# Fetching f, k and q in rows of four tokens: 64 token groups stand twice on the partitions

## The chip, the cores and the metric

The kernel runs on one core of one Trainium2 chip. The metric is the device time of one execution in microseconds (us). The kernel before took 827.85 us, the median of three runs (826.41 to 830.13).

## What is computed

Three layers follow each other. The first, and the only one that the change touches, is a gated linear attention over 4 batches, 8 heads, 768 tokens and 48 channels per head:

```python
f = 1.0 / (1.0 + np.exp(-f_logit))
state = np.zeros((B, H, D, D), dtype=np.float32)
for t in range(S):
    state = f[:, :, t, :, None] * state + np.einsum('bhd,bhe->bhde', k[:, :, t], v[:, :, t])
    y[:, :, t] = np.einsum('bhd,bhde->bhe', q[:, :, t], state)
```

Its output, as 3072 rows of 384 values, goes to a mixture of 8 experts (each takes 384 tokens, in the order of a gate's logits) and then to a dense layer with a gated activation. All inputs are float32, in HBM. f, k, q and v lie as [batch, head, token, channel], so that neighbouring tokens of one head are neighbours in memory and heads are 768 x 48 values apart.

## The kernel before

The attention function works on units of U=256 tokens of one batch (12 units, three per batch), each as two chunks of 128 tokens (24 chunks, j in the code). Its instructions are written out by hand, engine by engine: the loop over j interleaves the matrix work of chunk j with the preparation of unit j//2+2, by small closures (`slot`, `refill`). Every engine runs its own queue strictly in the order written. DMAs of this part are all issued by SP, in order: `later` collects the loads and the stores of x that are issued at the next flush.

**Loading and regrouping (L62 to L87).** `load` brings one unit of f, k or q into a tile `fr`, `kr` or `qr` [128, 8 heads, 96]: partition p holds tokens 2p and 2p+1 of the unit, which are 96 values or 384 bytes in one piece, for each head. Each of the three tiles has one buffer, so the next unit's load is issued only when the readers of the present one are done. f goes through Tanh (L77) and a scale (L78) on ACT into `ft`; DVE multiplies the f of the two tokens (L79) into `pmf`; k and q are spread into `pmk` and `pmq` as two planes, one for each of the two tokens: in one, k is multiplied by the second token's f (L82) and q by the first's (L86), and the other plane is copied by ACT (L83, L87). In these tiles a pair of heads fills 2 x 64 columns (48 used).

**Transposing and scaling.** PE transposes each [128 groups, pair of heads] block into `pT` in PSUM: `decays` for f (L92), `turned` for k and q (L113), the two planes interleaved. DVE scans the products of f along the tokens (L99, L107) and scales q and k with them (L126). What follows works on transposed tiles [channels of a pair, tokens]: scores (L146), the state's part of y (L152), y (L203), the update of the state (L214 to L222).

**Output.** `l_mm` (L228) turns y back to [tokens, 384] and computes the gate's logits in the same product; ACT copies y out (L233), SP stores it to `x_dram` (L234). Beside all this SP also loads v (L71) and, for the layers behind, the weights `pw` (L947) and `wo` (L966), which DVE, ACT and POOL unpack a piece per slot.

The change touches `load`, `decay`, `keys`, `queries`, `decays`, `turned`, the head number in `y_mm` and `kv_mm`, the copy in `l_mm` and the gate weight's load at L240. Everything behind `x_dram` stays.

Of the kernel before, what the change touches and what calls it, by code (L numbers as in the profile page):

```python
# [17 lines left out]
def attention(tc, q,k,v,f,wg, x_dram, lg, ident, pmin, ranges, prep, setup, spin):  # L18
    nc=tc.nc
    ctx=ExitStack()  # L20
    with ctx:
        ld=ctx.enter_context(tc.tile_pool(name="ald",bufs=2))
        cs=ctx.enter_context(tc.tile_pool(name="acs",bufs=1))
        wk=ctx.enter_context(tc.tile_pool(name="awk",bufs=2))
        ps=ctx.enter_context(tc.tile_pool(name="aps",bufs=1,space=PS))
        perm={'f':cs.tile([128,NP,2,64],F32,name="pmf")}
        nc.vector.memset(perm['f'][:,:,:,48:],1.0)
        for nm in 'kq':
            t=cs.tile([128,2,NP,2,64],F32,name=f"pm{nm}")
            nc.vector.memset(t[:,:,:,:,48:],0.0)  # L30
            perm[nm]=t
        half=cs.tile([128,1],F32,name="half"); nc.vector.memset(half,0.5)
        ft=cs.tile([128,2,H,D],F32,name="ft")
        L=G+1; W2=4*L
        held=ps.tile([128,512],F32,name="pC"); m0=held[:,:W2-1]; m1=held[:,512-W2:]
        nc.vector.memset(held,0.0)
# [15 lines left out]
        FF=[]
        for i in range(2):
            t=cs.tile([128,W2+4],F32,name=f"ff{i}"); nc.gpsimd.memset(t,0.0); FF.append(t)
        for t in VP: nc.gpsimd.memset(t[:,:,:,D:],0.0)
        nc.gpsimd.memset(SW,0.0)
        for s in range(2):
            for o in range(2):
                b=(s^o)*D
                nc.gpsimd.tensor_copy(SW[64*s:64*s+48,o::2,b:b+D],ident[64*s:64*s+48,None,64*s:64*s+D].to_broadcast([48,NP//2,D]))  # L60
        raw={}
        def load(u,nm,h0=0,h1=H):  # L62
            b,o=divmod(u*U,S)
            if nm!='v':
                src={'f':f,'k':k,'q':q}[nm]
                t=ld.tile([128,H,2*D],F32,name=nm+"r",bufs=1) if h0==0 else raw[nm,u]
                nc.sync.dma_start(t[:,h0:h1],bass.AP(tensor=src.tensor,offset=src.offset+b*H*S*D+h0*S*D+o*D,ap=[[2*D,128],[S*D,h1-h0],[1,2*D]]))
            else:
                t=VP[u%2]
                for c in range(2):  # L70
                    nc.sync.dma_start(t[:,c,:,:D],bass.AP(tensor=v.tensor,offset=v.offset+b*H*S*D+(o+c*C)*D,ap=[[D,C],[S*D,H],[1,D]]))  # L71
            raw[nm,u]=t
        view=lambda u,nm: raw[nm,u].rearrange("p h (r d) -> p r h d",d=D)
        home=lambda nm,r: perm[nm][:,r].rearrange("p a s d -> p (a s) d")[:,:,:48]
        def decay(u,i,h0=0,h1=H):
            x=ft[:,:,h0:h1]
            if i==0: nc.scalar.activation(x,view(u,'f')[:,:,h0:h1],AF.Tanh,scale=0.5)  # L77
            elif i==1: nc.scalar.activation(x,x,AF.Identity,bias=half[:,0:1],scale=0.5)  # L78
            else: nc.vector.tensor_mul(perm['f'].rearrange("p a s d -> p (a s) d")[:,h0:h1,:48],ft[:,0,h0:h1],ft[:,1,h0:h1])  # L79
        def keys(u,i,h0=0,h1=H):  # L80
            x=view(u,'k')[:,:,h0:h1]
            if i==0: nc.vector.tensor_mul(home('k',0)[:,h0:h1],x[:,0],ft[:,1,h0:h1])  # L82
            else: nc.scalar.copy(home('k',1)[:,h0:h1],x[:,1])  # L83
        def queries(u,i,h0=0,h1=H):
            x=view(u,'q')[:,:,h0:h1]
            if i==0: (nc.vector if u else nc.gpsimd).tensor_tensor(out=home('q',0)[:,h0:h1],in0=x[:,0],in1=ft[:,0,h0:h1],op=OP.mult)  # L86
            else: nc.scalar.copy(home('q',1)[:,h0:h1],x[:,1])  # L87
        KH={};QT={};PC={};PX={};SX={}
        V=nc.vector
        def decays(u,pairs):  # L90
            pt=ps.tile([128,512],F32,name="pT",bufs=PB).rearrange("p (a c g) -> p a c g",a=NP,c=2)
            for p in pairs: nc.tensor.transpose(pt[:,p].rearrange("p c g -> p (c g)"),perm['f'][:,p].rearrange("p a d -> p (a d)"),ident)  # L92
            for h in sorted({p//2 for p in pairs}):
                ff=FF[h][:,:W2].rearrange("p (a c g) -> p a c g",a=2,c=2)
                nc.scalar.copy(ff[:,:,:,1:],pt[:,2*h:2*h+2])
        flat=lambda t: t.rearrange("p a c g -> p (a c g)")
# [10 lines left out]
            V.tensor_tensor_scan(flat(SX[u,h])[:,1:][:,::-1],FF[h][:,2:W2+1][:,::-1],m1[:,1:][:,::-1],0.0,op0=OP.mult,op1=OP.max)  # L107
        PT={}
        def turned(u,nm,h):
            pt=ps.tile([128,512],F32,name="pT",bufs=PB).rearrange("p (a g r) -> p a g r",a=2,r=2)  # L110
            for a in range(2):
                for r in range(2):
                    nc.tensor.transpose(pt[:,a,:,r],perm[nm][:,r,2*h+a].rearrange("p s d -> p (s d)"),ident)  # L113
            PT[u,nm,h]=pt
        def scaled(u,nm,h):
            if nm=='k': o=KH[u]=KHB[u%2]
            elif h==0: o=QT[u]=wk.tile([128,NP,U],F32,name="qt")
# [20 lines left out]
        AM={};KT={};pA={}  # L138
# [51 lines left out]
        def y_mm(j,part):  # L190

            u,c=divmod(j,2); first=j%6==0
            vr=raw['v',u]; last=j==NCH-1
            rows=[slice(64*s,64*s+64) for s in range(2)]
            if part==0:
                if last: PY[j]=[ps.tile([128,NP,C],F32,name=f"pA{i}") for i in range(2)]
                else: PY[j]=[ps.tile([128,NP,C],F32,name="pT",bufs=PB) for _ in range(1 if first else 2)]*(2 if first else 1)
                return
            yt=wk.tile([128,NP,C],F32,name="yt")
            for p in (0,2,1,3):  # L200
                py=PY[j][p%2]
                for s in range(2):
                    nc.tensor.matmul(py[rows[s^p%2],p],vr[:,c,2*p+s],AM[j][:,s,p],start=first,stop=first or p>1)  # L203
                if p>1 and not first: nc.scalar.copy(yt[:,p%2::2],py[:,p%2::2])
            if first: nc.scalar.copy(yt,py)
            YT[j]=yt
        def kv_mm(j):
            u,c=divmod(j,2); first=j%6==0
            if j%6==5 or j>=NCH: return
            vr=raw['v',u]  # L210
            pk=ps.tile([128,512],F32,name="pT",bufs=PB)[:,:NP*D].rearrange("p (a d) -> p a d",a=NP)
            for p in range(NP):
                for s in range(2):
                    nc.tensor.matmul(pk[64*s:64*s+64,p],KT[j][:,p,s],vr[:,c,2*p+s,:D],start=True,stop=True)  # L214
            sn=St[(j+1)%2][:,:,:D]; so=St[j%2][:,:,:D]
            def update():
                pcb=PC[u][:,:,c][:,:,None].to_broadcast([128,NP,D])
                if first:
                    nc.vector.tensor_tensor(out=sn,in0=pk,in1=pcb,op=OP.mult)
                else:  # L220
                    nc.vector.tensor_add(so,so,pk)
                    nc.gpsimd.tensor_tensor(out=sn,in0=so,in1=pcb,op=OP.mult)  # L222
            late.append(update)
        def l_mm(j):
            W=2*D+8
            px=ps.tile([128,512],F32,name="pT",bufs=PB)[:,:NP*W].rearrange("p (a e) -> p a e",a=NP)
            for p in (0,2,1,3):
                nc.tensor.matmul(px[:,p],YT[j][:,p],SW[:,p],start=True,stop=True)  # L228
            y=wk.tile([128,NP,2*D],F32,name="y")
            def logits(): nc.vector.tensor_reduce(lg[:,j],px[:,:,2*D:].rearrange("p a e -> p e a"),axis=AX.X,op=OP.add)  # L230
            if j==NCH-1: logits()
            else: late.append(logits)
            nc.scalar.copy(y,px[:,:,:2*D])  # L233
            later.append(lambda: nc.sync.dma_start(x_dram[j*C:(j+1)*C,:],y.rearrange("p a d -> p (a d)")))  # L234
        ranges=ranges(lambda: ps.tile([128,384],F32,name="pT",bufs=PB),lambda: ps.tile([128,512],F32,name="pT",bufs=PB))
        for h in (0,4):
            for nm in 'fqk': load(0,nm,h,h+4)
        load(0,'v')
        for s in range(2):
            for o in range(2): nc.sync.dma_start(SW[64*s:64*s+48,o::2,2*D:],wg.rearrange("(p s d) e -> s d p e",p=NP,s=2)[s^o][:,o::2])  # L240
        WARM=(4,1,8)
        def warm(n):

            t=ps.tile([128,512],F32,name="pT",bufs=PB)
            for _ in range(n): nc.tensor.matmul(t[:,:128],ident,ident,start=True,stop=True)
        warm(WARM[0])
        lo,hi=(0,4),(4,8)
        for i in range(3): decay(0,i,*lo)
        decays(0,(0,1))
        for i in range(2): queries(0,i,*lo)  # L250
# [19 lines left out]
        for nm in 'fqk': load(1,nm)  # L270
# [652 lines left out]
def gla_moe_ffn(tc,q,k,v,f_logit,moe_w_gate,moe_w1,moe_w2,moe2_w_in,moe2_w_out,out):  # L923
    nc=tc.nc
    with ExitStack() as ctx:
# [133 lines left out]
        with tc.tile_pool(name="prep",bufs=1) as pi:  # L1059
            attention(tc,q,k,v,f_logit,moe_w_gate,x_dram,lg,ident,pmin,ranges,both(prep_in(pi),prep_out(pi,wr0,0,NOUT,3,512)),lambda: (rt.constants(),p0),rt.spin)  # L1060
# [103 lines left out]
```

## Time and profile before

| | |
|---|---|
| median of three runs | 827.85 us |
| the profiled execution's own time | 825.67 us |
| its span, first to last instruction | 824.0 us |
| PE busy in the span | 789.4 us (96%) |
| DVE busy | 547.4 us (66%) |
| ACT busy | 365.4 us (44%) |
| q1 (SP's DMA queue): packets, bytes | 95872, 73.96 MB |

The attention part fills about the first 150 us. Shares over the whole span mix it with the expert layers, where PE is busy nearly all the time; what the change is worth is read from the first 150 us alone, engine by engine. A DMA share over 1 in a stretch means that packets of one DMA engine overlap.

### The profile page before, as it was taken

How to read it: one execution, taken by the hardware profiler on the slowest of the kernel's cores; microseconds unless marked ns; L12 is line 12 of the kernel's file. 1: busy time of each engine (PE TensorE's matmuls, PEld its weight loads, DVE VectorE, ACT ScalarE, POOL GpSimd, SP SyncE). 2: the span in 40 equal slices, each digit the busy share in tenths (PEclk: the TensorE clock that was granted, in tenths of full speed). 3: DMA queues.
4: the chain of work that ended last, by engine and by line, in shares of the span. 5: the costliest groups of instructions: out<-in, count | busy, mean ns of one | idle time of the engine just before them, and what ended most of it. 6: DMA issues, size and time to landing. Idle time of an engine off the chain costs nothing.

```text
span 824.0 us, 16675 instructions
## 1 busy us (share of the span) xinstructions
PE 789.4 (96%) x6385; PEld 757.4 (92%) x6385; DVE 547.4 (66%) x1517; ACT 365.4 (44%) x757; POOL 125.5 (15%) x215
## 2 busy tenths in 40 slices
PE   7989999879999999999999999999999999999994
PEld 6878898769999999899999999999999999999994
DVE  6999999767797468648855866587756524642431
ACT  5877786242455144415431643254235424541431
POOL 2556543120011001101010001100300020010001
PEclk9999999969999999999999999999999999999998
DMA  9999984550034013203322322322213332331000
GB/s 225 228 257 253 275 236 119 176 191 1 1 88 123 1 37 104 91 20 122 110 74 68 97 85 78 95 87 84 91 63 97 89 99 72 97 97 39 1 1 33
DMA packets 99032, 84.54 MB, mean 103 GB/s; under 512 B 67328, under 2 KB 86912, under 8 KB 98944
## 3 DMA queue, kind: packets, MB, share of 16 engines
q1 hardware_dynamic: 95872, 73.96, 31.9%
q0 software_dynamic: 3072, 9.44, 3.6%
q8 instruction: 52, 0.85, 0.4%
q14 instruction: 36, 0.29, 0.1%
HBM read 73.94 MB, written 9.44 MB: 101 GB/s over the span
## 4 chain that ended last, share of the span: by engine, by line
PE 59%; issue 10%; DVE 7%; DMA 2%; ACT 1%; POOL 1%; SPq 0%; POOLq 0%; DVEq 0%; ACTq 0%
PE acc L736 10%; PE pF L736 10%; PE acc L737 9%; PE acc L738 9%; PE pF L737 9%; PE pF L738 9%; DVE ga L881 1%; DVE hl L884 1%; DVE w1l L785 1%; PE pF L823 1%; POOL out_dram L915 1%; DMA xg<-x_dram,q_ids 1%; ACT hh L883 1%; DMA wst<-in_moe_w_dram 1%; DMA xh<-in_moe_w_dram 1%
## 5 line engine op out<-in xcount | busy, mean ns | idle before, releaser
L881 DVE SCALAR_TENSOR_TENSOR ga<-ga,pF 128x384 f32<-128x384 f32 x128 | 70.8, 553 | 100.0 <-ACT ga L879 99.6
L736 PE MATMUL acc<-wo,hh 128*128 128x384 f32 x384 | 132.9, 346 | 1.0 <-ACT hh L883 1.0
L736 PE MATMUL pF<-xh,wih 128*128 128x384 f32 x384 | 131.6, 343 | 0.0
L737 PE MATMUL acc<-wo,hl 128*128 128x384 f32 x384 | 129.6, 337 | 0.4 <-DVE hl L884 0.4
L737 PE MATMUL pF<-xh,wil 128*128 128x384 f32 x384 | 129.4, 337 | 0.0
L738 PE MATMUL acc<-wo,hh 128*128 128x384 f32 x384 | 129.3, 337 | 0.0
L738 PE MATMUL pF<-xl,wih 128*128 128x384 f32 x384 | 129.3, 337 | 0.0
L879 ACT ACTIVATE ga<-pF,three 128x384 f32<-128x384 f32 x128 | 74.3, 582 | 105.3 <-PE pF L738 101.0
L883 ACT CAST hh<-ga 128x384 fp32r<-128x384 f32 x128 | 65.8, 514 | 88.6 <-DVE ga L881 86.2
L844 ACT ACTIVATE hh<-pF 128x384 fp32r<-128x384 f32 x64 | 31.5, 492 | 131.5 <-PE pF L738 118.6
L915 POOL DMA_INDIRECT out_dram<-ga,q_ids x24 | 24.2, 1010 | 385.5 <-ACT ga L913 382.5
L884 DVE TENSOR_TENSOR hl<-ga,hh 128x384 fp32r<-128x384 f32 x128 | 71.0, 555 | 13.4 <-ACT hh L883 9.8
L845 DVE SCALAR_TENSOR_TENSOR hl<-pF,hh 128x384 fp32r<-128x384 f32 x64 | 35.5, 555 | 65.6 <-ACT hh L844 65.3
L736 PEld LDWEIGHTS acc<-wo,hh 128*128 128x128 f32 x384 | 72.1, 188 | 2.2 <-ACT hh L883 1.3
L737 PEld LDWEIGHTS acc<-wo,hl 128*128 128x128 f32 x384 | 72.2, 188 | 1.8 <-DVE hl L884 1.8
L737 PEld LDWEIGHTS pF<-xh,wil 128*128 128x128 f32 x384 | 72.2, 188 | 0.0
L736 PEld LDWEIGHTS pF<-xh,wih 128*128 128x128 f32 x384 | 72.2, 188 | 0.0
L738 PEld LDWEIGHTS pF<-xl,wih 128*128 128x128 f32 x384 | 72.1, 188 | 0.0
L738 PEld LDWEIGHTS acc<-wo,hh 128*128 128x128 f32 x384 | 72.0, 188 | 0.0
L736 PE MATMUL pF<-xh,w1h 128*128 128x384 f32 x192 | 66.6, 347 | 0.6 <-ACT xh L814 0.6
L736 PE MATMUL acc<-hh,w2h 128*128 128x384 f32 x192 | 66.1, 344 | 0.0
L737 PE MATMUL pF<-xh,w1l 128*128 128x384 f32 x192 | 64.8, 338 | 0.0
(285 smaller groups left out, 1605.9 us busy)
## 6 DMA issues: line engine op xcount, KB each, us to landing
wst<-in_moe_w_dram SPq DMA_DIRECT2D x58, 192.0 KB, 2.5
wst<-in_moe_w_dram SPq DMA_DIRECT2D x42, 256.0 KB, 2.9
pw<-in_moe_w_in_dram SPq DMA_DIRECT2D x12, 512.0 KB, 6.3
wo<-in_moe_w_out_dram SPq DMA_DIRECT2D x16, 384.0 KB, 7.3
pm<-in_moe_w_out_dram SPq DMA_DIRECT2D x32, 192.0 KB, 2.4
pm<-in_moe_w_in_dram SPq DMA_DIRECT2D x30, 192.0 KB, 2.5
v<-in_v_dram SPq DMA_DIRECT2D x24, 192.0 KB, 5.2
x_dram<-y SPq DMA_DIRECT2D x24, 192.0 KB, 4.5
```

The source lines that it names most:

```text
L736: nc.tensor.matmul(out, ahi, bhi, start=start, stop=False)
L737: nc.tensor.matmul(out, alo, bhi, start=False, stop=False)
L738: nc.tensor.matmul(out, ahi, blo, start=False, stop=stop)
L785: nc.vector.tensor_tensor(out=lo,in0=got[i],in1=hi.bitcast(F32),op=OP.subtract)
L823: nc.tensor.transpose(p[:,h*128:(h+1)*128],s.xg[:,h,d*128:(d+1)*128],s.ident)
L844: nc.scalar.activation(hh,p,AF.Relu)
L845: s.defer(2,lambda: nc.vector.scalar_tensor_tensor(hl,p,0.0,hh.bitcast(F32),op0=OP.max,op1=OP.subtract))
L879: nc.scalar.activation(a,p,AF.Relu,bias=s.three[:,0:1])
L881: late(f,n1,lambda: nc.vector.scalar_tensor_tensor(g,a,6.0,p,op0=OP.min,op1=OP.mult))
L883: late(f,n2,lambda: nc.scalar.copy(gh,g))
L884: late(f,n3,lambda: nc.vector.tensor_tensor(out=gl,in0=g,in1=gh.bitcast(F32),op=OP.subtract))
L915: st=nc.gpsimd.indirect_dma_start(out=s.out,out_offset=bass.IndirectOffsetOnAxis(ap=ids[:,t:t+1],axis=0),in_=o,in_offset=None)
```

## The change

f, k and q are fetched in rows of four tokens, 192 values or 768 bytes in one piece. A unit of 256 tokens has 64 such groups, and they stand twice on the partitions: partitions 0 to 63 hold heads 0 to 3, partitions 64 to 127 heads 4 to 7. So each load becomes two DMAs of 64 partitions and four heads each. A pair of heads for the transposes is now made of heads of one half, and a transposed block holds both halves side by side: `turned` does the four tokens of a group one by one, for two pairs at a time, and writes every fourth column of `pT` (every second before); `decays` writes every second column (each column before). The number of heads behind a pair and a side is `head(p,s)`; the copy of y puts the pairs back in the order of the output.

```diff
+        ft=cs.tile([128,4,4,D],F32,name="ft")
...
+        head=lambda p,s: 4*(p%2)+2*(p//2)+s
+        def load(u,nm,h0=0,h1=4):
...
-                t=ld.tile([128,H,2*D],F32,name=nm+"r",bufs=1) if h0==0 else raw[nm,u]
-                nc.sync.dma_start(t[:,h0:h1],bass.AP(tensor=src.tensor,offset=src.offset+b*H*S*D+h0*S*D+o*D,ap=[[2*D,128],[S*D,h1-h0],[1,2*D]]))
+                t=ld.tile([128,4,4*D],F32,name=nm+"r",bufs=1) if h0==0 else raw[nm,u]
+                for g in range(2):
+                    nc.sync.dma_start(t[64*g:64*g+64,h0:h1],bass.AP(tensor=src.tensor,offset=src.offset+b*H*S*D+(4*g+h0)*S*D+o*D,ap=[[4*D,64],[S*D,h1-h0],[1,4*D]]))
...
+        home=lambda nm,r: perm[nm][:,r::2,:,:48]
...
-            else: nc.vector.tensor_mul(perm['f'].rearrange("p a s d -> p (a s) d")[:,h0:h1,:48],ft[:,0,h0:h1],ft[:,1,h0:h1])
+            else: nc.vector.tensor_mul(perm['f'][:,:,h0:h1,:48],ft[:,0::2,h0:h1],ft[:,1::2,h0:h1])
...
-            if i==0: nc.vector.tensor_mul(home('k',0)[:,h0:h1],x[:,0],ft[:,1,h0:h1])
+            if i==0: nc.vector.tensor_mul(home('k',0)[:,:,h0:h1],x[:,0::2],ft[:,1::2,h0:h1])
...
-            for p in pairs: nc.tensor.transpose(pt[:,p].rearrange("p c g -> p (c g)"),perm['f'][:,p].rearrange("p a d -> p (a d)"),ident)
+            for h in halves:
+                for i in range(2):
+                    nc.tensor.transpose(pt[:,2*h:2*h+2].rearrange("p b c (g i) -> p b (c g) i",i=2)[:,:,:,i],perm['f'][:,i,2*h:2*h+2].rearrange("p s d -> p (s d)"),ident)
...
-            for a in range(2):
-                for r in range(2):
-                    nc.tensor.transpose(pt[:,a,:,r],perm[nm][:,r,2*h+a].rearrange("p s d -> p (s d)"),ident)
+            for i in range(4):
+                nc.tensor.transpose(pt.rearrange("p (a g i) -> p a g i",a=2,i=4)[:,:,:,i],perm[nm][:,i,2*h:2*h+2].rearrange("p s d -> p (s d)"),ident)
...
-            nc.scalar.copy(y,px[:,:,:2*D])
+            nc.scalar.copy(y.rearrange("p (b a) d -> p a b d",b=2),px[:,:,:2*D].rearrange("p (a b) d -> p a b d",b=2))
...
-        for h in (0,4):
-            for nm in 'fqk': load(0,nm,h,h+4)
+        for h in (0,2):
+            for nm in 'fqk': load(0,nm,h,h+2)
```

On PE, ACT, DVE and POOL the order and the number of instructions stay, only shapes and waits differ. On SP each load of f, k and q is now two issues. The first rows of SP's queue before (names are the tile written and the input read, then the shape written; the waits are for earlier DMAs, which share eight semaphores in turn, and for readers of the buffer):

```order
L67 DMA fr<-in_f_logit_dram 128x4x96
L67 DMA qr<-in_q_dram 128x4x96
L67 DMA kr<-in_k_dram 128x4x96
L67 DMA fr<-in_f_logit_dram 128x4x96
L67 DMA qr<-in_q_dram 128x4x96
L67 DMA kr<-in_k_dram 128x4x96
L71 DMA v_111<-in_v_dram 128x8x48 x2
L240 DMA sw<-in_moe_w_gate_dram 48x2x8 [waits DMAHW0_49,Pool_49]
L240 DMA sw<-in_moe_w_gate_dram 48x2x8 [waits DMAHW1_49]
L240 DMA sw<-in_moe_w_gate_dram 48x2x8 [waits DMAHW2_49]
L240 DMA sw<-in_moe_w_gate_dram 48x2x8 [waits DMAHW3_49]
L67 DMA fr<-in_f_logit_dram 128x8x96 [waits DMAHW4_49,Activation_49]
```

The same stretch of SP's queue now, from the second part of unit 0 to the load of f for unit 1 (line numbers are two to five higher there):

```order
L69 DMA fr<-in_f_logit_dram 64x2x192 x2
L69 DMA qr<-in_q_dram 64x2x192 [waits DMAHW0_49]
L69 DMA qr<-in_q_dram 64x2x192 [waits DMAHW1_49]
L69 DMA kr<-in_k_dram 64x2x192 [waits DMAHW2_49]
L69 DMA kr<-in_k_dram 64x2x192 [waits DMAHW3_49]
L73 DMA v_111<-in_v_dram 128x8x48 [waits DMAHW4_49]
L73 DMA v_111<-in_v_dram 128x8x48 [waits DMAHW5_49]
L244 DMA sw<-in_moe_w_gate_dram 48x2x8 [waits DMAHW6_49,Pool_49]
L244 DMA sw<-in_moe_w_gate_dram 48x2x8 [waits DMAHW7_49]
L244 DMA sw<-in_moe_w_gate_dram 48x2x8 [waits DMAHW0_49]
L244 DMA sw<-in_moe_w_gate_dram 48x2x8 [waits DMAHW1_49]
L69 DMA fr<-in_f_logit_dram 64x4x192 [waits DMAHW2_49,Activation_49]
```

Unit 0 takes twelve issues instead of six (in two parts of half the heads), and the v, gate and unit-1 loads stand behind them.

On DVE the same instructions stand in the same places; the ones that read `qr` and `kr` wait for two DMAs instead of one. Before, in the preparation of unit 2:

```order
L79 TENSOR_TENSOR pmf<-ft 128x8x48 [waits Activation_49]
L219 TENSOR_TENSOR St_117<-pT,pmin 128x4x48 [waits PE_49]
L937 TENSOR_SCALAR pm<-pw 128x512 [waits DMAHW7_49]
L86 TENSOR_TENSOR pmq<-qr,ft 128x8x48 [waits DMAHW2_49]
L126 TENSOR_TENSOR kh_114<-pT,S 128x512 [waits DVE_49,PE_49]
L939 SCALAR_TENSOR_TENSOR pm<-pw,pm 128x512 [waits DVE_49]
L82 TENSOR_TENSOR pmk<-kr,ft 128x8x48 [waits DMAHW3_49]
```

The same place now:

```order
L81 TENSOR_TENSOR pmf<-ft 128x8x48 [waits Activation_49]
L223 TENSOR_TENSOR St_117<-pT,pmin 128x4x48 [waits PE_49]
L941 TENSOR_SCALAR pm<-pw 128x512 [waits DMAHW0_49]
L88 TENSOR_TENSOR pmq<-qr,ft 128x2x4x48 [waits DMAHW5_49,DMAHW4_49]
L130 TENSOR_TENSOR kh_114<-pT,S 128x512 [waits DVE_49,PE_49]
L943 SCALAR_TENSOR_TENSOR pm<-pw,pm 128x512 [waits DVE_49]
L84 TENSOR_TENSOR pmk<-kr,ft 128x2x4x48 [waits DMAHW7_49,DMAHW6_49]
```

Nothing moved here; the shapes have one dimension more and two rows one wait more.

## Rows read from the trace of the kernel before

**Rows 1.** The page: DVE's busy tenths in 40 slices of the span; DMA packets by size.
```profile
DVE  6999999767797468648855866587756524642431
...
DMA packets 99032, 84.54 MB, mean 103 GB/s; under 512 B 67328, under 2 KB 86912, under 8 KB 98944
```

**Rows 2.** Busy time of each engine in two stretches of 25 us, clock, DMA share.
```profile
core 0: us, PE busy (x) PEld busy (x) DVE busy (x) ACT busy (x) POOL busy (x), PEclk, DMA share, GB/s
25.00:50.00 25.00, 24.36 (x468) 22.12 (x457) 24.86 (x50) 19.68 (x46) 16.27 (x25) 1.00 0.94 240
75.00:100.00 25.00, 22.59 (x382) 19.70 (x379) 23.86 (x52) 18.76 (x44) 15.23 (x22) 1.00 1.00 271
```

**Rows 3.** What DVE waited for, 25 to 150 us: total, times, longest.
```profile
DVE St L221 <- PE pT L214: 4.0, 6, 1.1
DVE pm L937 <- DMA wo<-in_moe_w_out_dram: 0.5, 1, 0.5
```

**Rows 4.** Timeline of SP, start of the kernel: start, duration (idle before, what ended it).
```profile
0.81 0.44 SPq L67 DMA_DIRECT2D fr<-in_f_logit_dram  x1
...
3.50 0.51 SPq L67 DMA_DIRECT2D kr<-in_k_dram  x1
4.05 2.41 SPq L71 DMA_DIRECT2D v<-in_v_dram  x2
6.57 2.53 SPq L240 DMA_DIRECT2D sw<-in_moe_w_gate_dram  x4
9.20 0.38 SPq L67 DMA_DIRECT2D fr<-in_f_logit_dram  x1
```

**Rows 5.** Timeline of ACT: the Tanh of f (units 1 and 2) and the step behind it.
```profile
12.87 0.84 ACT L77 ACTIVATE ft<-fr 128x768 f32<-128x768 f32 x1 [1.15 <-DMA fr<-in_f_logit_dram]
...
19.96 0.84 ACT L77 ACTIVATE ft<-fr 128x768 f32<-128x768 f32 x1 [1.40 <-DMA fr<-in_f_logit_dram]
...
41.41 0.94 ACT L78 ACTIVATE ft<-ft,half 128x768 f32<-128x768 f32 x1
```

**Rows 6.** Timeline of DVE: the product of f's two tokens (units 1, 2 and 4).
```profile
14.71 0.56 DVE L79 TENSOR_TENSOR pmf<-ft 128x384 f32<-128x384 f32 x1 [1.10 <-ACT ft L78]
...
22.15 0.56 DVE L79 TENSOR_TENSOR pmf<-ft 128x384 f32<-128x384 f32 x1 [0.66 <-ACT ft L78]
...
45.05 0.88 DVE L79 TENSOR_TENSOR pmf<-ft 128x384 f32<-128x384 f32 x1
```

**Rows 7.** DMA packets in 2.5:3.5 and 18.5:21.5 (f, k, q), and 15.25:17 (pw).
```profile
DMA packets 801, 0.30 MB, mean 298 GB/s; under 512 B 801, under 2 KB 801, under 8 KB 801
...
DMA packets 2052, 0.79 MB, mean 264 GB/s; under 512 B 2051, under 2 KB 2051, under 8 KB 2051
...
DMA packets 187, 0.70 MB, mean 400 GB/s; under 512 B 16, under 2 KB 16, under 8 KB 187
```

**Rows 8.** Transposes in 25:125, by line: busy, mean ns of one.
```profile
L113 PE MATMUL pT<-ident,pmq 128*128 128x128 f32 x72 | 11.3, 280 | 0.0
L92 PE MATMUL pT<-ident,pmf 128*128 128x128 f32 x32 | 4.9, 275 | 1.7 <-DVE pmf L79 1.0 <-ACT kt L187 0.7
```

**Rows 9.** Timeline of SP: the row on each side of two idle stretches.
```profile
35.38 0.71 SPq L234 DMA_DIRECT2D x_dram<-y  x1
38.53 0.34 SPq L947 DMA_DIRECT2D pw<-in_moe_w_in_dram  x1
...
47.03 0.54 SPq L234 DMA_DIRECT2D x_dram<-y  x1
50.28 0.34 SPq L947 DMA_DIRECT2D pw<-in_moe_w_in_dram  x1
```

**Rows 10.** Two instructions whose shapes change, 0 to 155 us, by line.
```profile
L86 DVE TENSOR_TENSOR pmq<-qr,ft 128x384 f32<-128x384 f32 x11 | 8.4, 759 | 0.0
...
L233 ACT COPY y<-pT 128x384 f32<-128x384 f32 x24 | 11.7, 488 | 4.7 <-PE pT L228 1.9 <-DVE lg L230 1.1 <-ACT yt L204 1.0
```

**Rows 11.** DMA issues of f, count, size, us to landing, 0 to 155 us.
```profile
fr<-in_f_logit_dram SPq DMA_DIRECT2D x11, 384.0 KB, 5.3
```

More of the change, by code (lines that the diff above doesn't have):

```diff
@@ L25, in attention @@
         ps=ctx.enter_context(tc.tile_pool(name="aps",bufs=1,space=PS))
-        perm={'f':cs.tile([128,NP,2,64],F32,name="pmf")}
+        perm={'f':cs.tile([128,2,NP,64],F32,name="pmf")}
         nc.vector.memset(perm['f'][:,:,:,48:],1.0)
         for nm in 'kq':
-            t=cs.tile([128,2,NP,2,64],F32,name=f"pm{nm}")
-            nc.vector.memset(t[:,:,:,:,48:],0.0)
+            t=cs.tile([128,4,NP,64],F32,name=f"pm{nm}")
+            nc.vector.memset(t[:,:,:,48:],0.0)
             perm[nm]=t
         half=cs.tile([128,1],F32,name="half"); nc.vector.memset(half,0.5)
-        ft=cs.tile([128,2,H,D],F32,name="ft")
+        ft=cs.tile([128,4,4,D],F32,name="ft")
         L=G+1; W2=4*L
@@ L61, in attention @@
         raw={}
-        def load(u,nm,h0=0,h1=H):
+        head=lambda p,s: 4*(p%2)+2*(p//2)+s
+        def load(u,nm,h0=0,h1=4):
             b,o=divmod(u*U,S)
@@ L73, in attention, with decay @@
         view=lambda u,nm: raw[nm,u].rearrange("p h (r d) -> p r h d",d=D)
-        home=lambda nm,r: perm[nm][:,r].rearrange("p a s d -> p (a s) d")[:,:,:48]
-        def decay(u,i,h0=0,h1=H):
+        home=lambda nm,r: perm[nm][:,r::2,:,:48]
+        def decay(u,i,h0=0,h1=4):
             x=ft[:,:,h0:h1]
@@ L78, in decay, with keys, queries @@
             elif i==1: nc.scalar.activation(x,x,AF.Identity,bias=half[:,0:1],scale=0.5)
-            else: nc.vector.tensor_mul(perm['f'].rearrange("p a s d -> p (a s) d")[:,h0:h1,:48],ft[:,0,h0:h1],ft[:,1,h0:h1])
-        def keys(u,i,h0=0,h1=H):
+            else: nc.vector.tensor_mul(perm['f'][:,:,h0:h1,:48],ft[:,0::2,h0:h1],ft[:,1::2,h0:h1])
+        def keys(u,i,h0=0,h1=4):
             x=view(u,'k')[:,:,h0:h1]
-            if i==0: nc.vector.tensor_mul(home('k',0)[:,h0:h1],x[:,0],ft[:,1,h0:h1])
-            else: nc.scalar.copy(home('k',1)[:,h0:h1],x[:,1])
-        def queries(u,i,h0=0,h1=H):
+            if i==0: nc.vector.tensor_mul(home('k',0)[:,:,h0:h1],x[:,0::2],ft[:,1::2,h0:h1])
+            else: nc.scalar.copy(home('k',1)[:,:,h0:h1],x[:,1::2])
+        def queries(u,i,h0=0,h1=4):
             x=view(u,'q')[:,:,h0:h1]
-            if i==0: (nc.vector if u else nc.gpsimd).tensor_tensor(out=home('q',0)[:,h0:h1],in0=x[:,0],in1=ft[:,0,h0:h1],op=OP.mult)
-            else: nc.scalar.copy(home('q',1)[:,h0:h1],x[:,1])
+            if i==0: (nc.vector if u else nc.gpsimd).tensor_tensor(out=home('q',0)[:,:,h0:h1],in0=x[:,0::2],in1=ft[:,0::2,h0:h1],op=OP.mult)
+            else: nc.scalar.copy(home('q',1)[:,:,h0:h1],x[:,1::2])
         KH={};QT={};PC={};PX={};SX={}
@@ L91, in decays @@
             pt=ps.tile([128,512],F32,name="pT",bufs=PB).rearrange("p (a c g) -> p a c g",a=NP,c=2)
-            for p in pairs: nc.tensor.transpose(pt[:,p].rearrange("p c g -> p (c g)"),perm['f'][:,p].rearrange("p a d -> p (a d)"),ident)
-            for h in sorted({p//2 for p in pairs}):
+            halves=sorted({p//2 for p in pairs})
+            for h in halves:
+                for i in range(2):
+                    nc.tensor.transpose(pt[:,2*h:2*h+2].rearrange("p b c (g i) -> p b (c g) i",i=2)[:,:,:,i],perm['f'][:,i,2*h:2*h+2].rearrange("p s d -> p (s d)"),ident)
+            for h in halves:
                 ff=FF[h][:,:W2].rearrange("p (a c g) -> p a c g",a=2,c=2)
@@ L109, in turned @@
         def turned(u,nm,h):
-            pt=ps.tile([128,512],F32,name="pT",bufs=PB).rearrange("p (a g r) -> p a g r",a=2,r=2)
-            for a in range(2):
-                for r in range(2):
-                    nc.tensor.transpose(pt[:,a,:,r],perm[nm][:,r,2*h+a].rearrange("p s d -> p (s d)"),ident)
-            PT[u,nm,h]=pt
+            pt=ps.tile([128,512],F32,name="pT",bufs=PB)
+            for i in range(4):
+                nc.tensor.transpose(pt.rearrange("p (a g i) -> p a g i",a=2,i=4)[:,:,:,i],perm[nm][:,i,2*h:2*h+2].rearrange("p s d -> p (s d)"),ident)
+            PT[u,nm,h]=pt.rearrange("p (a g r) -> p a g r",a=2,r=2)
         def scaled(u,nm,h):
@@ L202, in y_mm @@
                 for s in range(2):
-                    nc.tensor.matmul(py[rows[s^p%2],p],vr[:,c,2*p+s],AM[j][:,s,p],start=first,stop=first or p>1)
+                    nc.tensor.matmul(py[rows[s^p%2],p],vr[:,c,head(p,s)],AM[j][:,s,p],start=first,stop=first or p>1)
                 if p>1 and not first: nc.scalar.copy(yt[:,p%2::2],py[:,p%2::2])
@@ L213, in kv_mm @@
                 for s in range(2):
-                    nc.tensor.matmul(pk[64*s:64*s+64,p],KT[j][:,p,s],vr[:,c,2*p+s,:D],start=True,stop=True)
+                    nc.tensor.matmul(pk[64*s:64*s+64,p],KT[j][:,p,s],vr[:,c,head(p,s),:D],start=True,stop=True)
             sn=St[(j+1)%2][:,:,:D]; so=St[j%2][:,:,:D]
@@ L232, in l_mm @@
             else: late.append(logits)
-            nc.scalar.copy(y,px[:,:,:2*D])
+            nc.scalar.copy(y.rearrange("p (b a) d -> p a b d",b=2),px[:,:,:2*D].rearrange("p (a b) d -> p a b d",b=2))
             later.append(lambda: nc.sync.dma_start(x_dram[j*C:(j+1)*C,:],y.rearrange("p a d -> p (a d)")))
         ranges=ranges(lambda: ps.tile([128,384],F32,name="pT",bufs=PB),lambda: ps.tile([128,512],F32,name="pT",bufs=PB))
-        for h in (0,4):
-            for nm in 'fqk': load(0,nm,h,h+4)
+        for h in (0,2):
+            for nm in 'fqk': load(0,nm,h,h+2)
         load(0,'v')
         for s in range(2):
-            for o in range(2): nc.sync.dma_start(SW[64*s:64*s+48,o::2,2*D:],wg.rearrange("(p s d) e -> s d p e",p=NP,s=2)[s^o][:,o::2])
+            for o in range(2): nc.sync.dma_start(SW[64*s:64*s+48,o::2,2*D:],wg.rearrange("(o a s d) e -> s o d a e",o=2,a=2,s=2)[s^o][o])
         WARM=(4,1,8)
@@ L246, in attention @@
         warm(WARM[0])
-        lo,hi=(0,4),(4,8)
+        lo,hi=(0,2),(2,4)
         for i in range(3): decay(0,i,*lo)
```

## The prediction

> **What bounds the kernel now.** I read the page first, then the busy time by stretches, then what DVE waited for, then the timelines of the first 25 us, engine by engine, and last the DMA packets.
>
> The page's slices (20.6 us each) show DVE at nine tenths or more in the second to fourth, and 7 or more to the seventh [rows 1]. By stretches DVE is busy 24.86 of 25 us from 25 to 50, and 23.86 from 75 to 100, while ACT is at 19 to 20 and PE's weight loads at 20 to 22 [rows 2]. From 25 us on, what DVE waits for is PE and one load of `wo`, 4.5 us in all, and never f, k or q [rows 3]. So the attention part is bound by DVE's own instructions, in an order written by hand, from 25 us to its end. The DMA engines are nearly as full (0.94 and 1.00 [rows 2]), which makes the change look promising, but a full resource that nobody waits for is not the bound; 67328 of 99032 packets are under 512 bytes [rows 1].
>
> Before 25 us it is different. ACT's Tanh of f waits for the load in unit 1 (1.15 us) and unit 2 (1.40) [rows 5], and DVE behind it waits 1.10 and 0.66 us [rows 6]. Whatever shifts DVE there shifts all that follows, since DVE has no idle time later to win it back.
>
> **The change part by part.** The sum goes against the profiled execution: 825.67 us, 1.67 more than its span. The median of the runs shown is 2.18 us higher; I add that at the end.
>
> *Issues at the start.* From the first load of f at 0.81 us to v at 4.05 six loads are issued, 0.54 us each [rows 4]. Twelve take 6.48, so v comes at 7.29, 3.24 us late. Some of that comes back: v's two issues took 2.41 us and the gate weight's four 2.53, more than 0.54 each, which I read as a queue that was full behind 3072 packets; now there are half as many. At 0.54 each the six take 3.24 instead of 4.94. Unit 1's f is then issued at about 10.6 instead of 9.20, and its second half 0.43 later. Bounds: nothing comes back, 3.24 + 0.43 = 3.7 us late; or all eighteen issues take the 0.38 of the last row, and it is 0.4 us early. I take 1.4 + 0.43.
>
> *Packets.* With one size in flight the rate was 298 GB/s at 384 bytes and 400 at (nearly all) 4096 [rows 7]; over 16 engines that is 20.6 and 164 ns a packet. A line through both gives an estimate of 35 ns for 768 bytes against 41 for two of 384: 14% off a load's 1.32 us (393 KB at 298 GB/s), 0.19 us. Bounds: the lower is the full waits of unit 1 and 2 (rival C), the upper is rival B. Since the second half of a load is issued 0.43 us after the first, only half of the transfer is left behind it, which saves another 0.6: unit 1's f lands about 1.1 us later than now (1.83 - 0.19 - 0.6, rounded).
>
> *What that does to DVE.* Its instruction at 14.71 moves by 1.1 us. At 22.15 it had waited 0.66 for unit 2's f, so DVE itself is ready at 22.6; that f is asked for 1.1 later, and gets about 0.6 back from three shorter loads ahead of it and its own, so its data is ready near 22.65. The shift that remains is 0.5 us; bounds -1.8 (both waits gone) and 3.7.
>
> *The later units.* Each unit adds three issues of some 0.4 us to SP, 1.2 us. SP stands idle from 36.09 to 38.53 and from 47.57 to 50.28, 2.4 to 2.7 us a unit [rows 9], which hides it. What stands behind them in SP's queue are x, v and pw, for which DVE never waited [rows 3]. f may come later too: in unit 4 it was ready at 42.35 (41.41 + 0.94 [rows 5]) and used at 45.05 [rows 6], 2.7 us of cover. Without cover it would be 1.2 us for each of some nine units, 11 us.
>
> *Waits and shapes.* Two DVE instructions a unit wait for two DMAs instead of one, some 22 waits. The trace shows no price; nearest is the 0.11 us between SP's issues of v and the gate weight [rows 4], so 0 to 2.4 us. DVE has no idle time before L86 (0.0 in 11 instructions [rows 10]), so its sequencer runs ahead; I take 0.3. The copies and products keep their element counts and their runs of 48 values, so L86 (759 ns) and L233 (488) stay [rows 10]. For one more dimension the trace has no pair to compare; nearest are the transposes, 280 ns where every second column of PSUM is written and 275 where each is [rows 8], 2%: on three such DVE instructions of some 8.4 us a unit list, 0.5 us either way, 0 taken.
>
> *Transposes.* As many as before, 192 for k and q and 48 for f, now to every fourth and every second column. At 2% again that is about 1 us on PE, which has 2.9 to 5.3 us in each 25 without a weight load [rows 2]: nothing taken. The Trainium skill (SBUF — State Buffer, Door 1: The DMA port swizzle) says that PSUM has lines of 8 bytes and that any non-contiguous pattern slows matmuls significantly. At a step of two values the rows differ by 2% only; no run here shows a step of four. That is rival D.
>
> Sum: 0.5 + 0.3 = 0.8 us more, 826.5 for the profiled execution and 828.7 as a median. Its own range, 826 to 832, has the bounds of the start inside what is likely, and a median of three that moves by 1 us.
>
> **The rivals.**
>
> *B: a DMA that fills only 64 partitions is slower.* All loads of f, k, q, v and pw in the trace reach 128 partitions, so it shows no price; the bounds are 1 and 2 times the 1.32 us. For it speaks that the transfers are the fullest resource after DVE, against it that the worst stretch of f, k and q packets now (264 GB/s [rows 7]) is only 1.13 times slower than the best. At 1.6 times a load takes 0.8 us more. In the start four loads stand in a row before unit 2's Tanh: 3.2, with the 0.8 above 4.0 to 4.3 us, 832. Later three loads a unit cost 2.4, just under SP's 2.4 to 2.7 us idle and the 2.7 us of cover. It decides from 0.9 us a load on (2.7 over three, 1.7 times): each unit then loses the rest. At 2 times that is 4.0 - 2.7 = 1.3 us for nine units, and 5.8 at the start: 845. I price it at 833.
>
> The Trainium skill has a rule for just this (SBUF — State Buffer, Can I just issue two DMAs to hit both halves?): partitions 0 to 63 reach half of SBUF's DMA ports, and a second DMA on the other half, issued beside the first, added only 6%. Its table gives 196 GB/s for 64 partitions and 328 for 128, an estimate of 1.67 times, by which the time would be near 832 as well; no run here shows it yet.
>
> *C: the loads land sooner.* If halving the packets frees the queue more than I reckon, both DVE waits of the start go: 1.10 + 0.66 = 1.8 us less, 826. For it: DMA shares near 1 [rows 2]. Against: nobody waits for these loads later, and DVE's idle time (0.14 and 1.14 us in 25 [rows 2], some 3 us in all) bounds what else there is: at most 823.
>
> *D: the transposes to every fourth column take twice as long.* A transpose costs PE 157 ns (11.3 us over 72 [rows 8]); 192 of them doubled are 30 us. PE's weight loads leave about 20 us over the 125 us of this part, so 10 us show: 838. Against it, the 2% above.
>
> That the packets are not halved at all (the row of 768 bytes is cut again) would leave the issues without the gain: 829, inside the forecast.
>
> **How the numbers follow.** Forecast 0.55, B 0.24, C 0.15, D 0.06. What a measurement can tell from no change is 0.5%, 4.1 us: 823.7 to 832.0. Faster: only C's far end, 0.05. Slower: 0.05 of the forecast's bounds (nothing of the 3.24 us comes back, and the waits cost 2.4), 0.15 of B, 0.06 of D: 0.26. Same: 0.50 + 0.09 + 0.10 = 0.69. The range reaches from C's middle to D's price, 825 to 838; outside are half of C and the far ends of B and D, under 0.2.
>
> **What would show it right or wrong.** Packets under 512 bytes fall by about 18,400 to near 49,000, and 39 issues of f, k and q become 78. In the start, unit 1's f is issued near 10.6 and 11.0 us and DVE's L79 for it begins near 15.8, for unit 2 near 22.65. The time from issue to landing of f, 5.3 us now [rows 11], stays or falls. Later, DVE is as busy as now, and never waits for ACT's f. Rate B shows as fewer than 264 GB/s in a stretch with only f, k and q packets, and as DVE waiting on L80 in later units. Rival D shows as transposes well over 280 ns. I am wrong if DVE's total in the first 150 us changes by over 2 us without any of this.

## The result, and the profile after

The changed kernel took 838.99 us, the median of six runs (831.9 to 840.25), against 827.19 for the kernel before on the same chips: 1.0124 times as long, interval 1.0083 to 1.0164. It is slower, by 1.2%. The forecast of 828.7 and "no change" was wrong by 10 us; the time lies 1 us above the range and between rival B's price (833) and its far end (845). The profiled execution took 839.7 us with a span of 838.0, which is 14.0 more than before. The kernel before was profiled in one of its faster executions (825.67 us), so the traces differ by more than the medians do, which are 11.8 apart.

First the page of the changed kernel: DVE's busy tenths, and its DMA packets.

```profile
DVE  4999969877688557836965876667757534642431
...
DMA packets 81224, 84.55 MB, mean 101 GB/s; under 512 B 31088, under 2 KB 69104, under 8 KB 81136
```

The 36,864 packets of 384 bytes became 18,432 of 768: the total fell by 17,808, and those under 512 bytes by 36,240, since the new ones no longer count there. So the change does what it says. My "fall by 18,400 to near 49,000" took the fall of the total for that of the small ones.

Busy time by stretches, changed kernel (columns as in [rows 2]):

```profile
25.00:50.00 25.00, 24.21 (x448) 22.00 (x441) 23.79 (x48) 20.80 (x45) 13.82 (x25) 1.00 1.02 220
75.00:100.00 25.00, 23.64 (x407) 20.94 (x407) 24.02 (x48) 17.96 (x41) 15.18 (x22) 1.00 1.04 243
100.00:125.00 25.00, 19.64 (x305) 17.50 (x303) 16.43 (x38) 14.53 (x35) 7.82 (x15) 0.86 0.81 193
```

Against [rows 2] the DMA engines' share rose from 0.94 and 1.00 to 1.02 and 1.04 while the rate fell from 240 and 271 to 220 and 243 GB/s: fewer packets, and more time in them. From 100 to 125 us DVE is busy 16.43 us only; before it was 23.16:

```profile
100.00:125.00 25.00, 25.00 (x453) 23.30 (x452) 23.16 (x54) 19.98 (x46) 9.71 (x29) 1.00 0.92 236
```

What was waited for, 25 to 150 us, changed kernel (total, times, longest):

```profile
ACT ft L79 <- DMA fr<-in_f_logit_dram: 10.5, 6, 2.7
DVE pm L941 <- DMA wo<-in_moe_w_out_dram: 5.8, 1, 5.8
DVE St L225 <- POOL am L183: 2.7, 1, 2.7
DVE pmf L81 <- ACT ft L80: 1.1, 1, 1.1
```

In [rows 3] DVE lost 0.5 us to `wo`; now 5.8, and f is late for ACT six times. To see where the time went, follow one instruction of each unit, DVE's product of f (L79 before, L81 now). Three more rows of it before, for units 5, 8 and 9:

```profile
57.34 1.53 DVE L79 TENSOR_TENSOR pmf<-ft 128x384 f32<-128x384 f32 x1
...
93.82 1.22 DVE L79 TENSOR_TENSOR pmf<-ft 128x384 f32<-128x384 f32 x1
...
104.08 0.55 DVE L79 TENSOR_TENSOR pmf<-ft 128x384 f32<-128x384 f32 x1
```

and DVE's timeline of the changed kernel:

```profile
18.65 0.56 DVE L81 TENSOR_TENSOR pmf<-ft 128x384 f32<-128x384 f32 x1 [2.97 <-ACT ft L80]
...
27.12 0.56 DVE L81 TENSOR_TENSOR pmf<-ft 128x384 f32<-128x384 f32 x1 [1.07 <-ACT ft L80]
63.10 0.55 DVE L81 TENSOR_TENSOR pmf<-ft 128x384 f32<-128x384 f32 x1
...
100.81 0.97 DVE L81 TENSOR_TENSOR pmf<-ft 128x384 f32<-128x384 f32 x1
109.98 0.36 DVE L941 TENSOR_SCALAR pm<-wo 128x384 uint32<-128x384 uint32 x1 [5.75 <-DMA wo<-in_moe_w_out_dram]
116.66 0.55 DVE L81 TENSOR_TENSOR pmf<-ft 128x384 f32<-128x384 f32 x1
119.90 0.35 DVE L225 TENSOR_TENSOR St<-St,pT 128x192 f32<-128x192 f32 x1 [2.68 <-POOL am L183]
```

It is late by 3.94 us in unit 1 and 4.97 in unit 2 (14.71 and 22.15 in [rows 6]), 5.76 in unit 5, 6.99 in unit 8, and 12.58 in unit 9, behind the wait for `wo`; ACT's last copy of y ends 14.4 later. So the loss has two parts: 5.0 us in the start, 9.4 later. The second part does not come in equal shares: units 3 to 8 add 2.0 us, unit 9 with the wait for `wo` adds 5.6, and what follows 1.8. Meanwhile SP's queue falls further behind than DVE. It issues the first loads of `wo` 9.92 us late, as these rows show, before and now:

```profile
92.62 1.47 SPq L966 DMA_DIRECT2D wo<-in_moe_w_out_dram  x3
```

```profile
102.54 1.44 SPq L970 DMA_DIRECT2D wo<-in_moe_w_out_dram  x3
```

The start, SP's timeline of the changed kernel (x2 is a pair of DMAs):

```profile
0.81 1.40 SPq L69 DMA_DIRECT2D fr<-in_f_logit_dram  x2
2.25 1.26 SPq L69 DMA_DIRECT2D qr<-in_q_dram  x2
...
8.75 1.22 SPq L73 DMA_DIRECT2D v<-in_v_dram  x2
10.09 2.21 SPq L244 DMA_DIRECT2D sw<-in_moe_w_gate_dram  x4
12.39 1.26 SPq L69 DMA_DIRECT2D fr<-in_f_logit_dram  x2
...
17.67 1.26 SPq L69 DMA_DIRECT2D fr<-in_f_logit_dram  x2
```

A DMA of 64 partitions takes SP 0.63 us, where one of 128 took 0.38 to 0.51 [rows 4], so unit 1's f is issued at 12.39 us instead of 9.20, and unit 2's at 17.67 instead of 13.74 (the row below):

```profile
13.74 0.38 SPq L67 DMA_DIRECT2D fr<-in_f_logit_dram  x1
```

These 3.93 us are most of the 4.97 that DVE is late in unit 2. ACT's timeline shows what follows, and something I had not foreseen:

```profile
4.36 1.28 ACT L79 ACT_TABLE_LOAD   x1 [4.36 <-DMA fr<-in_f_logit_dram]
...
16.80 0.84 ACT L79 ACTIVATE ft<-fr 128x768 f32<-128x768 f32 x1 [3.02 <-DMA fr<-in_f_logit_dram]
24.93 0.84 ACT L79 ACTIVATE ft<-fr 128x768 f32<-128x768 f32 x1 [1.76 <-DMA fr<-in_f_logit_dram]
```

The table load (a row of its own ahead of the first Tanh, 1.28 us) began at 0.81 us before, beside the first DMA:

```profile
0.81 1.28 ACT L77 ACT_TABLE_LOAD   x1 [0.81 <-PEq L1153]
```

The first Tanh now waits for two DMAs, and the load of its table stands behind one of these waits.

### The profile page after: what moved, and what is told of

Read it like the earlier page. It is cut to its first block, busy times and chain, and to the rows that moved or that the text cites. A ratio compares the mean times of both kernels' runs of the same rounds, so it can differ in the third digit from the quotient of the medians.

```text
span 838.0 us, 16765 instructions
## 1 busy us (share of the span) xinstructions
PE 795.7 (95%) x6385; PEld 762.8 (91%) x6385; DVE 548.0 (65%) x1517; ACT 365.0 (44%) x757; POOL 124.7 (15%) x215
## 4 chain that ended last, share of the span: by engine, by line
PE 61%; issue 9%; DVE 5%; DMA 1%; ACT 1%; POOL 1%; SPq 0%; POOLq 0%; DVEq 0%; ACTq 0%
PE pF L740 10%; PE acc L740 10%; PE acc L741 10%; PE pF L741 10%; PE pF L742 10%; PE acc L742 10%; DVE ga L885 1%; DVE hl L888 1%; PE pF L827 1%; POOL out_dram L919 1%; ACT hh L887 1%; DMA xg<-x_dram,q_ids 1%; DVE w1l L789 1%; DMA xh<-in_moe_w_dram 0%; PE pR L530 0%
```

## The experiments

Two causes were to be told apart: the rate of a DMA that fills one half of the partitions (rival B), and the issues, twice as many and dearer, on SP.

**One suspect at a time, in the kernel before.** `e1_halves` fetches each load by two DMAs of the lower and the upper 64 partitions, still 384 bytes a row; `e2_heads` by two DMAs of all 128 partitions with half the heads each; `e5_evenodd` by two DMAs of the even and the odd partitions.

```diff
-                nc.sync.dma_start(t[:,h0:h1],...,ap=[[2*D,128],[S*D,h1-h0],[1,2*D]]))
+ e1:            for g in range(2): nc.sync.dma_start(t[64*g:64*g+64,h0:h1],...+64*g*2*D,ap=[[2*D,64],[S*D,h1-h0],[1,2*D]]))
+ e2:            for h in (h0,h0+n): nc.sync.dma_start(t[:,h:h+n],...,ap=[[2*D,128],[S*D,n],[1,2*D]]))   # n=(h1-h0)//2
+ e5:            for g in range(2): nc.sync.dma_start(t[g::2,h0:h1],...+g*2*D,ap=[[4*D,64],[S*D,h1-h0],[1,2*D]]))
```

> The kernel before, with nothing changed but that each load of f, k and q is two DMAs of 64 partitions (rows of 384 bytes stay). If the loss comes from SP's issues (78 instead of 39, some 0.63 us each), it takes what the changed kernel takes: 836 to 840, unit 1's f issued near 12.4 us. If it comes from slow transfers into 64 partitions, also slower, 836 to 845, and the rate of f, k, q packets falls under 220 GB/s in a stretch with only them. If it comes from the regrouping (transposes to every fourth column, shapes), it stays at 827 to 830.

> The kernel before, each load of f, k and q as two DMAs of all 128 partitions and half of the heads. Issues theory: as many issues as in the changed kernel, so 835 to 840. Theory of slow transfers into 64 partitions: all partitions are reached, so 828 to 831 (the start alone, 2 us, since ACT's table load then stands behind the wait for the first of two DMAs).

> The kernel before, each load of f, k and q as two DMAs of 64 partitions, the even ones and the odd ones (rows of 384 bytes stay). As many issues, each of the same shape as with lower and upper half, but every DMA reaches all over the partitions. If the loss with halves comes from where the 64 partitions lie, the mean packet time of 384 bytes falls from 33 back to 25 ns and the time to that of two DMAs by heads: 830 to 833. If it comes from 64 partitions in a DMA or from the issues of that shape (0.63 us each against 0.48), it stays at 839 to 843.

**The same in the changed kernel.** `e6_interleaved` puts the two copies of the token groups on the even and the odd partitions; a transposed block is then read out with the two interleaved (in `turned`, shown, and likewise in `decays`).

```diff
-                    nc.sync.dma_start(t[64*g:64*g+64,h0:h1],...)
+                    nc.sync.dma_start(t[g::2,h0:h1],...)
...
-                nc.tensor.transpose(pt.rearrange("p (a g i) -> p a g i",a=2,i=4)[:,:,:,i],...)
+                nc.tensor.transpose(pt.rearrange("p (a g i) -> p g a i",a=2,i=4)[:,:,:,i],...)
```

> The changed kernel with heads 0 to 3 on the even and heads 4 to 7 on the odd partitions, so that each DMA still fills 64 partitions, spread over all. If where the partitions lie decides, packets of 768 bytes take some 40 ns instead of 55 and the time falls by 8 to 11 us, to 828 to 831 (the two issues a load stay). If the issues decide, 836 to 839. If it is the regrouping, 839.

| DMAs of one load | 384 bytes a row | 768 bytes a row |
|---|---|---|
| one, 128 partitions | 827.2 to 828.4 (before) | |
| two, half the heads each | 830.78, 1.0040 [1.0020, 1.0059] (e2) | |
| two, even and odd partitions | 834.27, 1.0067 [1.0035, 1.0099] (e5) | 831.53, 1.0043 [1.0023, 1.0063] (e6) |
| two, lower and upper half | 842.32, 1.0195 [1.0168, 1.0222] (e1) | 838.99, 1.0124 [1.0083, 1.0164] (after) |

(Medians in us; ratios to the kernel before on the same chip, with their intervals.) From halves to even and odd, with the same count of issues and bytes, 7.5 to 8.1 us go by the medians in either column; by the ratios, which compare better because the runs were on different chips, it is some 7 to 11 us. The rows of 768 bytes are worth 2.7 to 3.3 us by the medians, 2 to 6 by the ratios; between e5 and e6 the intervals overlap. A second issue (e2) costs 3, though not by the issue alone: ACT's table load stands behind a wait there too (3.94 us). e5 came 1.3 us above the 830 to 833 expected of it, e6 0.5 above its 828 to 831.

The reason is in stretches of the traces that hold hardly any other packets. Each row is from another kernel; first e1, 23 to 26 us:

```profile
DMA packets 1665, 0.64 MB, mean 212 GB/s; under 512 B 1664, under 2 KB 1664, under 8 KB 1664
```

e5, 22.5 to 25.5 us:

```profile
DMA packets 2134, 0.85 MB, mean 285 GB/s; under 512 B 2121, under 2 KB 2121, under 8 KB 2133
```

The changed kernel, 23 to 26 us:

```profile
DMA packets 875, 0.65 MB, mean 217 GB/s; under 512 B 49, under 2 KB 874, under 8 KB 874
```

e6, 22.5 to 24.5 us:

```profile
DMA packets 852, 0.68 MB, mean 341 GB/s; under 512 B 53, under 2 KB 835, under 8 KB 851
```

Into one half the rate is 212 GB/s at 384 bytes and 217 at 768. Spread over all partitions it is 285 (264 in [rows 7]) and 341, but these two stretches also hold 12 and 16 packets of 4096 bytes, which lift the rate. Steadier is the mean time of one packet of f, k or q over a whole trace: at 384 bytes 24.7 ns before, 24.9 in e2, 24.7 in e5 and 32.8 in e1; at 768 bytes 41.9 in e6 and 55.3 in the changed kernel. So the place costs a factor of 1.33 at 384 bytes and 1.32 at 768, and a packet of 768 takes 15 to 16% less than two of 384 in either place. What this does to the DMA engines, over the same 75 us (25 to 100) of three kernels, first the kernel before, then the changed one, then e6 (packets, MB, and the time of the packets as a share of 16 engines):

```profile
q1 hardware_dynamic: 36953, 19.03, 95.8%
```

```profile
q1 hardware_dynamic: 26791, 17.49, 101.5%
```

```profile
q1 hardware_dynamic: 28025, 17.72, 86.1%
```

The changed kernel keeps the engines longer for fewer bytes; e6 leaves room. And in e6 DVE's later waits for loads are gone, and one of ACT's is left, 1.8 us in unit 5 (25 to 150 us, as above; the other, of 2.7, is the start's, in unit 2):

```profile
ACT ft L79 <- DMA fr<-in_f_logit_dram: 4.5, 2, 2.7
DVE St L225 <- PE pT L218: 4.4, 6, 1.8
```

`wo` is not among DVE's waits any more, and the product of f is 5.56 us late in unit 2 and 5.57 in unit 5 (27.71 and 62.91); in unit 9 it is 7.10 (111.18). So after the start e6 loses little, but in the start it loses as much as the changed kernel, with faster packets. (Its profiled execution, 835.3 us, was the slowest of ten, so this trace shows more loss than the median.)

**The waits that the trace names, one by one, in the changed kernel.** `e3_table` runs a Tanh of one value ahead, so that the table is there; `e4_wo_early` issues the first three loads of `wo` six loads earlier (`ahead` starts what fetches `wo`; its edit is shown in part).

```diff
+ e3:        once=cs.tile([128,1],F32,name="once"); nc.scalar.activation(once,half,AF.Tanh)
+ e4:                if i==10 and ahead: ahead()
```

> The changed kernel with a Tanh of one value per partition ahead of the loads, so that ACT's table load does not stand behind the wait for f. ACT's first Tanh of f starts near 4.4 instead of 5.66 us and DVE's first product of f near 5.6 instead of 6.86; if the start carries through, 1.3 us faster than the changed kernel, 837.5. If DVE's later waits for loads decide alone, no change of the time, 839.

> The changed kernel with the first three loads of wo issued six loads earlier in SP's queue. If the 5.75 us that DVE waits for wo near 104 us come from SP's queue being late, that wait goes and the time falls by 5 to 7 us, to 832 to 834. If the DMA engines are the bound, the wait turns up at f, q or k of the next units and the time falls by under 2 us.

e3 took 836.31 us, 1.0116 [1.0089, 1.0142]; e4 836.36, 1.0107 [1.0078, 1.0136]: neither is told from the changed kernel. DVE's timeline of e3, units 0 and 1 (L82 there):

```profile
5.70 0.36 DVE L82 TENSOR_TENSOR pmf<-ft 128x192 f32<-128x192 f32 x1 [3.20 <-ACT ft L81]
...
18.63 0.56 DVE L82 TENSOR_TENSOR pmf<-ft 128x384 f32<-128x384 f32 x1 [3.97 <-ACT ft L81]
```

Unit 0 comes 1.2 us earlier (6.86 in the changed kernel), unit 1 no earlier (18.65), since its f is issued no earlier: the table is hidden behind the issues. In e4 the wait for `wo` is gone, and others stand in its place (25 to 150 us):

```profile
ACT ft L79 <- DMA fr<-in_f_logit_dram: 12.5, 8, 2.9
DVE pmq L88 <- DMA qr<-in_q_dram: 2.7, 2, 2.0
DVE pm L941 <- DMA pw<-in_moe_w_in_dram: 1.9, 2, 1.6
```

So the lateness moved to other loads in the queue; this change of order did not take it away.

**The start.** `e7_interleaved_table` is e6 with e3's line. `e8_act_issues` is e7 with the first three second halves issued by ACT. `f1_gate_later` is the kernel before with the gate weight's four DMAs behind unit 2's loads; `f2_both` is e8 with that.

```diff
+ e8:  (nc.scalar if g>u+h0 else nc.sync).dma_start(t[g::2,h0:h1],...)
-        for s in range(2):
-            for o in range(2): nc.sync.dma_start(SW[64*s:64*s+48,o::2,2*D:],...)
...
         while later: later.pop(0)()
+        for s in range(2):
+            for o in range(2): nc.sync.dma_start(SW[64*s:64*s+48,o::2,2*D:],...)
```

> The same with the Tanh of one value ahead, so that ACT's table load stands before the wait for f. Unit 0's first product of f on DVE 1.2 us earlier; unit 1's still stands behind SP's twelve first issues, so 0 to 1 us faster than without.

> The same, and the three first second halves (f, q and k of unit 0) issued by ACT beside SP. SP's queue is three issues of 0.63 us shorter in the start, 1.9 us: unit 1's f is issued near 10.5 instead of 12.4 us, and the time falls by 1 to 2 us, to 826 to 829, if SP's issues set the start. If the transfers set it, no change.

> The kernel before with the gate weight's four DMAs, which stand in SP's queue between v and unit 1's f, issued after the loads of unit 2. If SP's queue sets when unit 1's f arrives, it is issued near 7.1 instead of 9.20 us, ACT and DVE of unit 1 start 1.1 us earlier and that carries through DVE's full queue to the end: 0.8 to 1.8 us faster, 826 to 827. If later waits take it back, no change, 827.7.

> Even and odd partitions, the table load ahead, three issues on ACT, and the gate weight later: what the experiments point to, in one. Unit 1's f is issued near 8.2 instead of 10.5 us. By SP's queue 2 us faster than without the gate weight's move, 828.5; with both extra costs gone and 768 bytes a packet it could meet the kernel before (827.7), and beat it only if the loads of later units cost it nothing.

e7 took 832.09 us, 1.0036 [1.0017, 1.0055]; e8 830.56, 1.0030 [1.0009, 1.0051]; f1 827.47 against 826.78, 1.0012 [0.9995, 1.0030]; f2 832.02, 1.0062 [1.0037, 1.0086]. No version beats the kernel before. e8 issues unit 1's f at 10.51 us instead of 12.4 and cuts unit 1's lateness to 1.42 us (16.13) and unit 2's to 3.08 (25.23), from 5.56 in e6; its median is 1.5 us below e7's, but the intervals overlap. f2, for which 828.5 was hoped, is no faster than e8: unit 1 comes another 1.04 us earlier (15.09), unit 2 no earlier (25.55). f1's DVE shows the same:

```profile
13.66 0.56 DVE L79 TENSOR_TENSOR pmf<-ft 128x384 f32<-128x384 f32 x1
22.19 0.56 DVE L79 TENSOR_TENSOR pmf<-ft 128x384 f32<-128x384 f32 x1 [1.27 <-ACT ft L78]
```

Unit 1 is 1.05 us earlier than in [rows 6], and unit 2 no earlier: it waits for its f. In f1 and f2 what moving the gate weight wins in unit 1 is given back in unit 2.

## Why the prediction was wrong

- *Issues at the start: mis-sized.* I took 0.54 us an issue, from rows with 128 partitions. Measured: twelve issues from 0.81 to 8.75 us, 0.66 each, and 3.64 us for the six behind them where I took 3.24. 1.46 and 0.40 us more make 12.39 of 10.53, which I had called about 10.6. It came 3.19 us late, next to the 3.24 that I had named for nothing coming back, and that is chance: 1.51 us did come back (from v's issue to that of unit 1's f it took 5.15 us before, 3.64 now), and dearer issues took 1.46 of it. My other bound was wrong in itself: eighteen issues of 0.38 us make it 1.1 us early, not 0.4.
- *"The shift that remains is 0.5 us": wrong.* Unit 2 is 4.97 us late, 3.93 of it because its f is issued so much later. I let it get 0.6 us back from shorter loads (four times 0.19 would be 0.8); the loads were longer, 1.81 us (393 KB at 217 GB/s) for 1.32. But that is not what decides here: e6, with faster packets, is 5.56 us late in unit 2.
- *Later units hidden: this step failed, and for B.* That the extra issues hide in SP's idle time was nearly right: e6 has as many, and falls back 1.5 us from unit 2 to unit 9. That a slower load hides there too was not. I let SP's 2.4 to 2.7 us idle a unit be the cover for B, but it is the DMA engines that have to find the time, and they stood at 0.94 and 1.00 in the row that I had quoted [rows 2]: an estimate of 0 to 0.7 us free in a unit of some 12. Three loads longer by 0.5 us are 1.5; the excess, an estimate of 0.8 to 1.5 us for some nine units, is 7 to 13 us, and 9.4 came. The size fits, but DVE did not lose it unit by unit: 2.0 us up to unit 8, then 5.6 at one load that came too late, `wo`. So "decides from 0.9 us a load on" was wrong: 0.5 us sufficed. And I dismissed `wo` because DVE waited only 0.5 us for it [rows 3]; a wait of 0.5 says that there is no cover at all.
- *B itself was right* in its direction and in what slows down, and had 0.24, but its account was not. I priced it at 1.6 times; by the packets it is 1.33 and 1.32. Its 4.0 to 4.3 us in the start were to come from slow loads; the 5.0 us there go with the issues, since e6 loses as much, and e3, with the table load out of the way, 4.92. Its later units were to hide up to 1.7 times and did not. That the time lies between its 833 and its 845 is in part luck. Of its signs, the rate came as written, 217 GB/s, under 264. From 25 us on DVE waited on L80 only once, in unit 2; in later units it is ACT that waits for f, five times, and DVE for `wo`. The Trainium skill's rule (SBUF — State Buffer, Can I just issue two DMAs to hit both halves?), by which two DMAs on the two halves do not make one of 128 partitions, agrees with e1: 32.8 ns a packet for 24.7. That section also says that only one transfer over all 128 partitions reaches all ports. No run shows the ports, but e5's pairs of 64, each on every second partition, took 24.7 ns a packet, as single DMAs of 128 did, so for the rate the measurement decides against asking for a single transfer. The factor of 1.67, an estimate from the Trainium skill's table (SBUF — State Buffer, Door 1: The DMA port swizzle), stands beside 1.33 and 1.32 here.
- *Packets: right in proportion.* I took 35 ns for 768 bytes against 41 for two of 384, 14% less. Over whole traces it is 41.9 ns in e6 against 49.4 for two of 24.7, 15% less; both are longer than in the clean stretches that I had used. On the halves a packet of 768 takes 55.3.
- *Transposes (rival D): right at nothing.* Changed kernel, 25 to 125 us, by line:

```profile
L117 PE MATMUL pT<-ident,pmk 128*128 128x128 f32 x60 | 9.6, 282 | 0.1
L97 PE MATMUL pT<-ident,pmf 128*128 128x128 f32 x32 | 4.9, 275 | 0.7 <-DVE pmf L81 0.7
```

  Every fourth column costs 282 ns, every second 275, against 280 and 275 in [rows 8]. The Trainium skill's rule (SBUF — State Buffer, Door 1: The DMA port swizzle), by which PSUM has lines of 8 bytes and a non-contiguous pattern slows matmuls significantly, is not borne out: 282 ns at a step of four values, 275 without one.
- *Rival C* (loads sooner) fell: ACT's L79 begins at 16.80 and 24.93 us, at 12.87 and 19.96 before [rows 5]. DVE's products with a second wait show no price of it, and L237 takes 492 ns for 488 [rows 10]. The product of q (L86 before, L88 now), which I had left at its price, takes 886 ns on average for 758 (25 to 170 us), but not by its shape: with the old shape e1 shows 981, with the new one e8 778.

## What to carry to other kernels

Count a transfer's packets and also the partitions that it fills: two DMAs on the two halves lost here more than rows twice as long gave. When a resource that nobody waits for is as full as the DMA engines here (95.8% from 25 to 100 us), its cover is the few per cent that are free, not the idle time of the queue that feeds it. And price each extra DMA by an issue of its own shape, above all where the first loads of a kernel stand in a row.

## What the runs showed that was not expected

- On SP a DMA of 64 partitions costs 0.63 us, whether its rows have 384 or 768 bytes, though it has fewer rows than those of 128 partitions that cost 0.38 to 0.51. Why, no run shows.
- A second wait ahead of the first Tanh moved its table load from 0.81 to 4.36 us. A Tanh of one value ahead brings it back to 0.81 (e3).
- The mean granted clock fell to 0.86 from 100 to 125 us, in part the lower of the two levels (1.2 and 2.4 GHz). Ahead of that PE stood idle behind DVE's wait for `wo`: it is busy 19.64 us there, and was 25.00 at 1.00 before.
